# Turning the first q and k on the matrix engine and loading three batches ahead: sliding-window attention and a feed-forward layer

## The chip, the cores and the metric

The kernel runs on one core of a Trainium2 chip. The metric is the device time of one execution in microseconds (us). A core has five engines that work side by side, each in the order of its own instructions: PE (matrix multiply; its weight loads are shown apart as PEld), DVE (vector), ACT (scalar functions), POOL (general) and SP, which only issues transfers here. An engine starts an instruction when those that it needs on other engines have signalled, and everything behind it on the same engine waits with it. Transfers run on 16 DMA engines.

## The reference, cut to what matters

```python
# q, k, v: (8, 8, 576, 64) float32; w_in (512, 2048), w_out (2048, 512)
window, dilation = 32, 4
scores = 1/sqrt(64) * q @ k^T                       # per batch and head
rel = pos[:, None] - pos[None, :]
plain = (rel >= 0) & (rel < 32)                      # heads 0 to 3
dil   = (rel >= 0) & (rel < 128) & (rel % 4 == 0)    # heads 4 to 7
attn = softmax(where(mask, scores, -1e9)) @ v
x = attn.transpose(0, 2, 1, 3).reshape(4608, 512)
h = x @ w_in
out = maximum(0.01 * h, h) @ w_out                   # (4608, 512) float32
```

## The kernel before

**Attention.** The work is cut into 16 half-batches, called batches from here on and counted by `n`: four heads of one of the 8 batch entries, plain windows for even `n`, dilated ones for odd `n`. A batch has four units `u` (two pairs of heads, two halves of 288 tokens). `scores(u)` multiplies k by q on PE for both heads (six or eight small matmuls), takes the exponential on ACT (`er`) and the mask on DVE (`em`). `values(u)` multiplies by v (`o`) and by ones (`den`), takes the reciprocal (for units 0 to 7 as exp(-ln) on ACT, later on DVE) and writes `xT`, the attention output with the model dimension on the partitions, in float16. The tiles `sps`, `o` and `den` have one buffer each.

**Where q and k come from.** The scores need q and k with the head dimension on the partitions. `load(n)` brings q, k and v in float32, q and k in runs of one 64-element row (256 bytes); `cast(n)` turns them into float16 on POOL (two instructions each for q and k, one for v); `transpose(n)` has two DMA transposes write `qT` and `kT`, of which there are two sets, one for even and one for odd `n`.

**Feed-forward.** The 4608 tokens form nine chunks `c` of 512. A chunk has 32 pieces: 16 `ff_in` (four matmuls into `hp`, then a leaky relu on ACT into `gt`) and 16 `ff_out` (four matmuls each into `op`; after every fourth, ACT copies the result to `ob` and SP stores it). From chunk 0 on, a unit is woven into every four pieces: with piece `i` of chunk `c`, at `i % 4 == 0` come the scores of the next unit and, by the unit's place in its batch, the cast of the next batch, the load of the batch after it or the transpose of the next; at `i % 4 == 2` come the values. So chunks 0 to 6 hold eight units each (8 to 63), and units 0 to 7 run ahead of the feed-forward. A chunk needs the `xT` of its own 512 tokens. The eight weight blocks (1 MB each) are loaded into a staging tile with two buffers and cast on DVE.

**What sets the order.** The order is written out by hand: each engine takes its instructions in the order in which the program names them. SP issues everything from one queue: loads, transposes and output stores.

Of the kernel before, what the change touches and what calls it, by code (L numbers as in the profile page):

```python
# [14 lines left out]
WIN = 32  # L15
# [9 lines left out]
def _masks_np():  # L25
    krel = np.arange(128)[:, None]
    c = np.arange(S)[None, :]
    key = 96 * (c // 96) - 32 + krel
    rel = c - key
    plain = (key >= 0) & (rel >= 0) & (rel < WIN)  # L30
    tau, ql = c // HALF, c % 72
    uq = 72 * tau + ql
    uk = 72 * tau - 32 + krel
    dil = (uk >= 0) & (uq - uk >= 0) & (uq - uk < WIN)
    return np.concatenate([plain, dil], axis=1).astype(np.float16)


@with_exitstack
def kernel(ctx: ExitStack, tc: tile.TileContext, q, k, v, w_in, w_out, out):
# [12 lines left out]
    mask_d = nc.inline_tensor(_masks_np(), name="masks").ap()  # L52

# [3 lines left out]
    mask = cst.tile([128, 2, 2, HALF], FP16, name="mask")  # L57
    xT = cst.tile([128, 4, NTOK], FP16, name="xT")

    NQK = 3  # L60
    qT = [cst.tile([128, PAD + 2 * S + PAD], FP16, name=f"qT{i}") for i in range(2)]
    kT = [cst.tile([128, PAD + 2 * S + PAD], FP16, name=f"kT{i}") for i in range(2)]
# [10 lines left out]
    def load(n):  # L73
        b, kind = divmod(n, 2)
        base = (b * H + 4 * kind) * S * D
        for nm, x in (("q", q), ("k", k)):
            t = stg.tile([96, 24, D], FP32, tag=nm + "f")
            nc.sync.dma_start(t, rows_ap(x, base, [[D, 96], [96 * D, 24], [1, D]]))  # L78
            qkf[n, nm] = t
# [24 lines left out]
    def cast(n, eng):  # L104
        kind = n % 2
        for nm in ("q", "k"):
            t = att.tile([96, 2, 6, 2, D], FP16, tag=nm + "h")
# [6 lines left out]
        t = att.tile([128, 32, D], FP16, tag="vh")  # L114
        m = 32 if kind else 24
# [3 lines left out]
    def transpose(n):  # L119
        for nm, dst in (("q", qT), ("k", kT)):  # L120
            o = dst[n % 2][:, PAD:PAD + 2 * S].rearrange("p (c r) -> p c r", r=96)
            nc.sync.dma_start_transpose(  # L122
                o, qkh.pop((n, nm)).rearrange("p a t h d -> p (a t h d)"))

# [3 lines left out]
    def scores(u):  # L128
# [4 lines left out]
        for j in range(4 if kind else 3):  # L133
            w = 72 if kind else 96
            for hh in range(2):
                r = slice(64 * hh, 64 * hh + 64)
                if kind:
                    ka = kT[n % 2][r, tok - 128 + j: tok - 128 + j + 512: 4]
                    qa = qT[n % 2][r, tok + j: tok + j + 288: 4]
                else:  # L140
                    ka = kT[n % 2][r, tok + 96 * j - 32: tok + 96 * j + 96]
                    qa = qT[n % 2][r, tok + 96 * j: tok + 96 * j + 96]
# [4 lines left out]
        m = mask[:, kind, half, :]  # L147
        mb = bass.AP(tensor=m.tensor, offset=m.offset, ap=[m.ap[0], [0, 2], m.ap[1]])
        nc.vector.tensor_tensor(out=em, in0=er, in1=mb, op=ALU.mult)  # L149
# [53 lines left out]
    def ff_in(c, j):  # L203
        if j == 0:
            gts[c] = moe.tile([128, 16, CH], FP16, tag="gt", name="gt")
# [52 lines left out]
    cast(2, P)  # L258
    transpose(2)
    cast_w(0, 2, V)  # L260
    load_w(1, 0)
    cast_w(0, 3, V)
    load_w(1, 1)
    load(3)
    cast_w(1, 0, V)
    load_w(1, 2)
    cast_w(1, 1, V)
    load_w(1, 3)
    scores(8)
    NU = 8 * B  # L270
    u = 8
    for c in range(9):
        pieces = list(ff_pieces(c))
        for i, f in enumerate(pieces):
            if u < NU:
                if i % 4 == 0:
                    if u + 1 < NU:
                        scores(u + 1)
                    n = u // 4
                    if u % 4 == 0 and n + 1 < 2 * B:  # L280
                        cast(n + 1, P)
# [42 lines left out]
```

## Time and profile before

| | us |
|---|---|
| median of three timed runs | 433.36 (431.92 to 435.08) |
| the profiled execution | 427.88 |
| its span, first to last instruction | 426.1 |
| PE busy in the span | 326.3 (77%) |
| DVE busy | 190.8 (45%) |
| ACT busy | 152.0 (36%) |
| POOL busy | 80.9 (19%) |

The span is what the profile divides; 1.8 us of the profiled execution lie around it. A matmul is pipelined, so that busy time of PE is not all work. The granted clock is the share of PE's full clock that was given. In a group of instructions the columns are busy time and mean nanoseconds of one, then the idle time of the engine just before them and what ended it. In a chain and a timeline they are start, duration and what it was; a bracket gives the idle time before and its releaser. "L219" is line 219 of the kernel, and PE's names are those of the tiles.

### The profile page before, as it was taken

To read this page: it belongs to the slowest core of one execution; us is meant where nothing else is said; L and a number is where in the kernel's file an instruction comes from. 1 tells how busy PE (TensorE), PEld (TensorE's weight loads), DVE (VectorE), ACT (ScalarE), POOL (GpSimd) and SP (SyncE) were. 2 spreads that over 40 slices of the span, in tenths; PEclk is the share of its full clock that TensorE was granted. 3 is DMA by queue.
4 is the path that set the end of the run, shared out by engine and by line. 5 is a ranking of instruction groups with operands and counts; after the bars stand their busy time and mean duration, and the time that the engine had idled before them with its cause. 6 is when DMAs were issued, how large, how long until landed. Compare 5 with 4: busy or idle time off the path is not lost.

```text
span 426.1 us, 5328 instructions
## 1 busy us (share of the span) xinstructions
PE 326.3 (77%) x2176; PEld 138.0 (32%) x2176; DVE 190.8 (45%) x192; ACT 152.0 (36%) x261; POOL 80.9 (19%) x91
## 2 busy tenths in 40 slices
PE   0033455892999499958996799859894999999996
PEld 0022122340334134423342243314341444444442
DVE  0027355462567346653765366717571666400000
ACT  1044323420362136312641164206521562451631
POOL 4605033202131313131313131213111100000000
PEclk9999998898899879997999699969997999999999
DMA  9999999559482929192909291758366301101001
GB/s 215 268 281 282 231 305 330 101 132 209 94 172 67 272 63 205 37 263 67 240 12 259 69 234 33 183 157 201 65 142 196 82 0 51 50 2 74 25 26 74
DMA packets 154702, 61.43 MB, mean 144 GB/s; under 512 B 137677, under 2 KB 145845, under 8 KB 154677
## 3 DMA queue, kind: packets, MB, share of 16 engines
q1 hardware_dynamic: 154677, 61.09, 58.1%
q8 instruction: 17, 0.28, 0.3%
q14 instruction: 8, 0.07, 0.1%
HBM read 42.21 MB, written 9.44 MB: 121 GB/s over the span
## 4 chain that ended last, share of the span: by engine, by line
PE 45%; DMA 33%; SPq 9%; POOL 4%; ACT 3%; DVE 2%; issue 2%; POOLq 0%; ACTq 0%
PE op L219 24%; DMA t<-in_k_dram 19%; PE hp L208 15%; DMA kT<-t 13%; SPq L78 4%; POOL t L112 4%; PE sps L143 3%; PE o L163 2%; DMA t<-in_v_dram 2%; SPq L122 2%; ACT ob L223 2%; PE den L166 1%; SPq L224 1%; DVE w L198 1%; DVE xT L178 1%
## 5 line engine op out<-in xcount | busy, mean ns | idle before, releaser
L219 PE MATMUL op<-w,gt 128*128 128x512 f16 x576 | 144.8, 402 | 0.0
L208 PE MATMUL hp<-xT,w 128*128 128x512 f16 x576 | 139.1, 389 | 0.1
L174 DVE RECIPROCAL rec<-den 128x288 f32<-128x288 f32 x56 | 109.6, 1958 | 60.8 <-PE den L166 60.7
L210 ACT ACTIVATE gt<-hp 128x512 f16<-128x512 f32 x144 | 86.0, 597 | 63.1 <-PE hp L208 62.1
L143 PE MATMUL sps<-qT,kT 64*128 64x72 f16 (+1 forms) x448 | 25.3, 237 | 77.0 <-DMA kT<-t 74.5
L112 POOL CAST t<-t 96x768 f16<-96x768 f32 x64 | 52.7, 850 | 151.6 <-DMA t<-in_q_dram 137.6
L219 PEld LDWEIGHTS <-gt 128*128 128x128 f16 x576 | 54.0, 102 | 69.1 <-issue 12.2
L149 DVE TENSOR_TENSOR em<-er,mask 128x576 f16<-128x576 f16 x64 | 32.3, 506 | 95.1 <-ACT er L145 94.9
L208 PEld LDWEIGHTS <-w 128*128 128x128 f16 x576 | 52.7, 99 | 64.8 <-issue 5.9
L145 ACT ACTIVATE er<-sps 128x576 f16<-128x576 f32 x64 | 41.5, 649 | 71.7 <-PE sps L143 71.7
L223 ACT COPY ob<-op 128x512 f32<-128x512 f32 x36 | 21.1, 586 | 127.7 <-PE op L219 127.7
L143 PEld LDWEIGHTS <-kT 64*128 64x128 f16 x448 | 14.1, 111 | 103.2 <-DMA kT<-t 60.1
L116 POOL CAST t<-t 128x1536 f16<-128x1536 f32 (+1 forms) x16 | 26.9, 1682 | 99.6 <-PE o L163 48.6
L163 PE MATMUL o<-em,t 128*64 128x72 f16 (+1 forms) x448 | 22.4, 222 | 19.2 <-DVE xT L181 7.9
L163 PEld LDWEIGHTS <-t 128*64 128x64 f16 x448 | 14.6, 119 | 46.8 <-issue 29.1
L178 DVE TENSOR_TENSOR xT<-o,rec 128x288 f16<-128x288 f32 x32 | 25.6, 800 | 4.4 <-ACT rec L172 3.4
L166 PE MATMUL den<-em,ones 128*64 128x288 f16 x128 | 21.2, 322 | 0.0
L181 DVE TENSOR_TENSOR xT<-o,rec 128x288 f16<-128x288 f32 x32 | 14.6, 457 | 4.1 <-ACT rec L172 3.1
L198 DVE CAST w<-t 128x2048 f16<-128x2048 f32 x8 | 9.8, 1231 | 13.2 <-DMA t<-in_moe_w_out_dram 13.2
L166 PEld LDWEIGHTS <-ones 128*64 128x64 f16 x128 | 8.5, 124 | 0.0
L171 ACT ACTIVATE ln<-den 128x288 f32<-128x288 f32 x8 | 3.3, 411 | 7.7 <-PE den L166 7.7
L172 ACT ACTIVATE rec<-ln 128x288 f32<-128x288 f32 x8 | 3.5, 442 | 0.3
(10 smaller groups left out, 3.1 us busy)
## 6 DMA issues: line engine op xcount, KB each, us to landing
t<-in_q_dram SPq DMA_DIRECT2D x16, 576.0 KB, 4.9
t<-in_k_dram SPq DMA_DIRECT2D x16, 576.0 KB, 6.8
out_dram<-ob SPq DMA_DIRECT2D x36, 256.0 KB, 2.4
t<-in_v_dram SPq DMA_DIRECT2D x7, 1024.0 KB, 8.5
t<-in_v_dram SPq DMA_DIRECT2D x7, 768.0 KB, 7.4
t<-in_moe_w_in_dram SPq DMA_DIRECT2D x4, 1024.0 KB, 6.0
t<-in_moe_w_out_dram SPq DMA_DIRECT2D x4, 1024.0 KB, 7.7
t<-in_v_dram SPq DMA_DIRECT2D x1, 896.0 KB, 8.3
```

Source lines behind the costliest of these rows:

```text
L112: eng(out=dst, in_=src)
L143: nc.tensor.matmul(sps[:, hh, w * j:w * j + w], ka, qa, start=True, stop=True)
L145: nc.scalar.activation(out=er, in_=sps[:, :, 0:HALF], func=AF.Exp, scale=SCALE)
L149: nc.vector.tensor_tensor(out=em, in0=er, in1=mb, op=ALU.mult)
L163: nc.tensor.matmul(o[64 * hh:64 * hh + 64, w * j:w * j + w], vt[:, sl, :], em[:, hh, w * j:w * j + w], start=True, stop=True)
L166: nc.tensor.matmul(den[64 * hh:64 * hh + 64, 0:HALF], ones, em[:, hh, :], start=True, stop=True)
L174: nc.vector.reciprocal(out=rec, in_=den[:, 0:HALF])
L178: nc.vector.tensor_tensor(out=x, in0=o[:, 0:HALF].rearrange("p (r u) -> p r u", r=4), in1=rec.rearrange("p (r u) -> p r u", r=4), op=ALU.mult)
L208: nc.tensor.matmul(hp, w1[j // 4][:, i, 128 * (j % 4):128 * (j % 4) + 128], xT[:, i, CH * c:CH * c + CH], start=(i == 0), stop=(i == 3))
L210: nc.scalar.activation(out=gts[c][:, j, :], in_=hp, func=AF.Prelu, alpha=0.01)
L219: nc.tensor.matmul(op, gts[c][:, j, 128 * t:128 * t + 128], w2[j // 4][:, j % 4, :], start=(j == 0), stop=(j == 15))
L223: nc.scalar.copy(out=ob, in_=op)
```

## The change

Batches 0 to 3 (the first two batch entries) no longer go through the DMA transposes: their q and k are loaded so that a partition holds six neighbouring tokens of a head (runs of 1.5 KB), and `pe_transpose` turns each pair of heads by six PE transposes against an identity into a PSUM tile `tp`, from which DVE or ACT copies to `qT` or `kT`, putting the tokens back in order. There are three sets of `qT` and `kT` instead of two, three buffers for the cast v instead of two, and one instead of two for the cast q and k and for `gt`. From batch 4 on, `prefetch` names the load three batches ahead, the cast two ahead and the DMA transpose two ahead (before: two, one and one). The masks are built on POOL instead of loaded, in a smaller tile that is read with a stride of zero. Four of the eight weight casts move from DVE to POOL. In chunk 0 no unit is woven into the first 16 pieces; units 8 to 15 come with the last 16, one for every two pieces.

```diff
-    mask_d = nc.inline_tensor(_masks_np(), name="masks").ap()
-    mask = cst.tile([128, 2, 2, HALF], FP16, name="mask")
+    mask = cst.tile([128, 3, 96], FP16, name="mask")
+    nc.gpsimd.memset(mask, 1.0)
+    nc.gpsimd.affine_select(out=mask, in_=mask, pattern=[[0, 3], [1, 96]], base=32,
+                            channel_multiplier=-1, compare_op=ALU.is_ge, fill=0.0)
+    nc.gpsimd.affine_select(out=mask, in_=mask, pattern=[[0, 3], [-1, 96]], base=-1,
+                            channel_multiplier=1, compare_op=ALU.is_ge, fill=0.0)
+    nc.gpsimd.memset(mask[0:32, 0, :], 0.0)
+    ident = cst.tile([96, 96], FP16, name="ident")
+    nc.gpsimd.memset(ident, 0.0)
+    nc.gpsimd.affine_select(out=ident, in_=ident, pattern=[[-1, 96]], base=0,
+                            channel_multiplier=1, compare_op=ALU.not_equal, fill=1.0)
...
-            nc.sync.dma_start(t, rows_ap(x, base, [[D, 96], [96 * D, 24], [1, D]]))
+            if n < NPE:
+                nc.sync.dma_start(t.rearrange("p (h t) d -> p h (t d)", h=4),
+                                  rows_ap(x, base, [[6 * D, 96], [S * D, 4], [1, 6 * D]]))
+            else:
+                nc.sync.dma_start(t, rows_ap(x, base, [[D, 96], [96 * D, 24], [1, D]]))
...
+    def pe_transpose(n, p, nm, eng):
+        h = qkh[n, nm]
+        o = (qT if nm == "q" else kT)[n % NB][:, PAD + S * p:PAD + S * p + S]
+        tp = psm.tile([128, 1024], FP16, tag="pm", name="tp")
+        for t in range(6):
+            nc.tensor.transpose(tp[:, 96 * t:96 * t + 96],
+                                h[:, p, t].rearrange("p h d -> p (h d)"), ident)
+        eng(out=o.rearrange("p (r t) -> p t r", t=6),
+            in_=tp[:, 0:S].rearrange("p (t r) -> p t r", t=6))
...
     load(0)
-    nc.sync.dma_start(mask, mask_d.rearrange("p (a b c) -> p a b c", a=2, b=2))
     load(1)
-    cast(0, P)
-    transpose(0)
-    load_w(0, 0)
-    load_w(0, 1)
-    cast(1, P)
-    transpose(1)
-    load(2)
+    for g in range(4):
+        load_w(0, g)
+    cast_qk(0, V, A)
+    cast_v(0, P)
+    for p in range(2):
+        pe_transpose(0, p, "q", V)
+        pe_transpose(0, p, "k", A)
+    cast_qk(1, P, P)
+    cast_v(1, P)
     scores(0)
     scores(1)
     for u in range(8):
+        if u == 2:
+            for p in range(2):
+                pe_transpose(1, p, "k", A)
+                pe_transpose(1, p, "q", V)
         if u + 2 < 8:
             scores(u + 2)
         values(u, True)
         if u == 3:
-            cast_w(0, 0, V)
-            load_w(0, 2)
+            cast_w(0, 0, P)
         if u == 4:
             cast_w(0, 1, V)
-            load_w(0, 3)
+            load_w(1, 0)
+            load_w(1, 1)
+        if u == 5:
+            cast_w(0, 2, P)
...
+    load_w(1, 2)
     cast_w(0, 3, V)
+    load_w(1, 3)
+    load(2)
     load(3)
...
+    def prefetch(n, slot):
+        if slot == 0 and n + 3 < 2 * B:
+            load(n + 3)
+        if slot == 1 and NPE <= n + 2 < 2 * B:
+            cast_qk(n + 2, P, P)
+            cast_v(n + 2, P)
+        if slot == 3 and NPE <= n + 2 < 2 * B:
+            transpose(n + 2)
...
+            if c == 0:
+                if i in (2, 4, 6, 8):
+                    g = (i - 2) // 2
+                    cast_w(1, g, V if g % 2 else P)
+                if i == 10:
+                    cast_qk(2, V, P)
+                    cast_v(2, P)
+                if i == 12:
+                    load(4)
+                    pe_transpose(2, 0, "q", V)
...
+                if i == 15:
+                    pe_transpose(2, 1, "k", V)
+                    scores(8)
+                    cast_qk(3, P, P)
+                    cast_v(3, P)
+                if 17 <= i <= 20:
+                    pe_transpose(3, (i - 17) // 2, "kq"[(i - 17) % 2], V)
+                per = 2
+                go = i >= 16
+            else:
+                per = 4
+                go = True
+            if go and u < NU:
+                if i % per == 0:
+                    if u + 1 < NU:
+                        scores(u + 1)
+                    prefetch(u // 4, u % 4)
+                if i % per == per // 2:
+                    values(u, False)
+                    u += 1
             f()
```

**SP's queue in the chunks.** One chunk's worth of SP's rows in the kernel before, around chunk 2; the numbers tell the tiles apart, and the kind of v load (L85 even, L95 odd) tells the batch.

```order
L78 DMA t_897<-in_q_dram 96x24x64
L78 DMA t_899<-in_k_dram 96x24x64
L85 DMA t_901<-in_v_dram 128x24x64
L122 DMA_TRANSPOSE qT1_81<-t_840 128x12x96
L122 DMA_TRANSPOSE kT1_83<-t_843 128x12x96
L224 DMA out_0_dram<-ob_1093 128x512
L78 DMA t_1109<-in_q_dram 96x24x64
L78 DMA t_1111<-in_k_dram 96x24x64
L95 DMA t_1113<-in_v_dram 128x8x256
L224 DMA out_0_dram<-ob_1147 128x512
L122 DMA_TRANSPOSE qT0_80<-t_1053 128x12x96
L122 DMA_TRANSPOSE kT0_82<-t_1056 128x12x96
```

The same stretch of SP's queue in the changed kernel, from the load at a chunk's start on:

```order
L79 DMA t_1405<-in_q_dram 96x24x64
L79 DMA t_1407<-in_k_dram 96x24x64
L96 DMA t_1409<-in_v_dram 128x8x256
L124 DMA_TRANSPOSE qT2_91<-t_1460 128x12x96
L124 DMA_TRANSPOSE kT2_94<-t_1463 128x12x96
L79 DMA t_1618<-in_q_dram 96x24x64
L79 DMA t_1620<-in_k_dram 96x24x64
L86 DMA t_1622<-in_v_dram 128x24x64
L245 DMA out_0_dram<-ob_1656 128x512
L245 DMA out_0_dram<-ob_1712 128x512
L245 DMA out_0_dram<-ob_1760 128x512
L124 DMA_TRANSPOSE qT0_89<-t_1672 128x12x96
```

The second load now stands right behind the first pair of transposes, ahead of the chunk's first store, and the second pair stands behind the third store; each pair is for the batch after next, where before it was for the next.

**DVE in chunk 0.** DVE's rows before, from the first units after unit 7 on (`w2` are weight casts, `rec` the reciprocals):

```order
L174 RECIPROCAL rec_452<-den_443 128x288
L181 TENSOR_TENSOR xT_79<-o_442,rec_452 128x288
L198 CAST w2_2_94<-t_394 128x2048
L149 TENSOR_TENSOR em_477<-er_475,mask_78 128x576
L198 CAST w2_3_95<-t_397 128x2048
L174 RECIPROCAL rec_508<-den_499 128x288
L181 TENSOR_TENSOR xT_79<-o_498,rec_508 128x288
```

DVE's rows in the changed kernel from piece 17 of chunk 0 on; `tp` are the turned q and k of batch 3:

```order
L135 COPY kT0_92<-tp_647 128x6x96
L195 RECIPROCAL rec_665<-den_656 128x288
L202 TENSOR_TENSOR xT_88<-o_655,rec_665 128x288
L135 COPY qT0_89<-tp_672 128x6x96
L170 TENSOR_TENSOR em_689<-er_687,mask_78 128x576
L135 COPY kT0_92<-tp_703 128x6x96
L195 RECIPROCAL rec_721<-den_712 128x288
L202 TENSOR_TENSOR xT_88<-o_711,rec_721 128x288
L135 COPY qT0_89<-tp_731 128x6x96
```

The weight casts are gone from between these units, four copies out of PSUM have come in, and the units that were spread over 32 pieces now come within 16.

**POOL at the start.** POOL's rows in the changed kernel behind the common opening:

```order
L41 MEMSET ones 128x64
L44 MEMSET mask 128x288
L45 ISA
L45 AFFINE_SELECT mask<-mask 128x288
L47 AFFINE_SELECT mask<-mask 128x288
L49 MEMSET mask 32x96
L51 MEMSET ident 96x96
L52 AFFINE_SELECT ident<-ident 96x96
```

Before, the memsets of `kT`'s edges followed at once on that of `ones`; now the masks and the identity, with one ISA row, stand ahead of them and of every cast on POOL.

More of the change, by code (lines that the diff above doesn't have):

```diff
@@ L22 @@
 CH = 512
[L25 to L35, printed above, removed]
 @with_exitstack
@@ L277 @@
                     if u + 1 < NU:
                         scores(u + 1)
-                    n = u // 4
-                    if u % 4 == 0 and n + 1 < 2 * B:
-                        cast(n + 1, P)
-                    if u % 4 == 1 and n + 2 < 2 * B:
-                        load(n + 2)
-                    if u % 4 == 2 and n + 1 < 2 * B:
-                        transpose(n + 1)
-                if i % 4 == 2:
+                    prefetch(u // 4, u % 4)
+                if i % per == per // 2:
@@ L289 @@
             f()
-            if c == 0 and i == 3:
-                cast_w(1, 2, V)
-            if c == 0 and i == 5:
-                cast_w(1, 3, V)
 _INS = ['q', 'k', 'v', 'moe_w_in', 'moe_w_out']
```

64 lines of the change are left out of this document (32 added, 32 removed).

## The prediction

> **What bounds the kernel now.** I read the busy time by stages first. The cuts are the first score matmul (21.4), the first feed-forward matmul (50.2), the start of chunk 1 (112.4), of chunk 6 (333.1) and of chunk 7 (367.3).
>
> ```profile
> core 0: us, PE busy (x) PEld busy (x) DVE busy (x) ACT busy (x) POOL busy (x), PEclk, DMA share, GB/s
> 0.00:21.40 21.40, 0.00 (x0) 0.00 (x0) 0.00 (x0) 1.28 (x1) 10.76 (x20) 1.00 1.03 241
> 21.40:50.20 28.80, 9.50 (x141) 6.03 (x141) 14.61 (x20) 12.19 (x25) 5.43 (x5) 1.00 1.03 260
> 50.20:112.40 62.20, 42.03 (x260) 16.59 (x259) 29.20 (x29) 16.51 (x29) 14.86 (x15) 0.89 0.77 200
> 112.40:333.10 220.70, 185.29 (x1280) 75.97 (x1279) 122.42 (x121) 82.03 (x141) 49.90 (x51) 0.92 0.62 146
> 333.10:367.30 34.20, 34.20 (x247) 14.60 (x246) 23.59 (x23) 15.58 (x27) 0.00 (x0) 1.00 0.16 49
> 367.30:422.60 55.30, 55.24 (x256) 24.85 (x254) 0.95 (x2) 23.79 (x40) 0.00 (x0) 1.00 0.10 39
> ```
>
> From 333.1 on PE is busy all the time at full clock. Chunk 6 has eight units of attention in it like chunks 1 to 5 and takes 34.20 us, while those five take 220.70 / 5 = 44.14 us each, at a granted clock of 0.92. So no engine's work sets chunks 1 to 5; a wait does. The waits of PE between 112.4 and 333 have a single row:
>
> ```profile
> PE sps L143 <- DMA kT<-t: 35.3, 10, 6.9
> ```
>
> Ten waits, two a chunk, 7.1 us a chunk; the other 2.5 us or so are the slow matmuls after each long one (0.92). The chain of waits leads from there to POOL's cast of k and a load. SP's own rows tell it otherwise:
>
> ```profile
> 252.67 1.60 POOL L112 CAST t<-t 96x768 f16<-96x768 f32 x2 [0.34 <-DMA t<-in_k_dram]
> 267.39 0.37 SPq L224 DMA_DIRECT2D out_dram<-ob  x1
> 267.81 0.43 SPq L78 DMA_DIRECT2D t<-in_q_dram  x1
> 270.56 2.89 SPq L95 DMA_DIRECT2D t<-in_v_dram  x1
> 274.50 2.72 SPq L122 DMA_TRANSPOSE qT<-t  x1
> 277.31 2.55 SPq L122 DMA_TRANSPOSE kT<-t  x1
> 282.00 0.42 PE L143 MATMUL sps<-qT,kT 64*128 64x96 f16 x6 [6.43 <-DMA kT<-t]
> ```
>
> The k that PE waits for at 282.0 was cast by 254.3. Its transpose is issued only at 277.3, because SP works in order and stands first at an output store that PE must earn (267.4), then spends 5.7 us on the next load. The wait is made by the queue, not by bandwidth: the DMA share is 0.62.
>
> **The change, part by part.** *Chunks 1 to 5.* In the new order of SP each pair of transposes belongs to the batch after next. With T the start of a chunk: SP issues the load by T+5.7, and the pair behind it (274.50 to 282.0: 7.5 us from issue to use) is usable at T+13.2; its scores come at piece 28 of 32, T+30.3. The second pair stands behind three stores, the third ready at about T+30.9, so usable at T+38.4; its scores come at piece 12 of the next chunk, T+47.6. Margins of 17 and 9 us, where today there are none. What is late next: q and k now have one cast buffer, so a cast waits for the transposes of the batch before, and the loop of cast and transposes is 4 x 0.85 + 7.5 = 10.9 us against 17.3 us per batch. DVE has slack, as a steady unit shows:
>
> ```profile
> 162.25 0.29 PE L166 MATMUL den<-em,ones 128*64 128x288 f16 x2
> 162.58 1.96 DVE L174 RECIPROCAL rec<-den 128x288 f32<-128x288 f32 x1 [0.81 <-PE den L166]
> 164.57 0.46 DVE L181 TENSOR_TENSOR xT<-o,rec 128x288 f16<-128x288 f32 x1
> 166.36 0.32 PE L163 MATMUL o<-em,t 128*64 128x96 f16 x6
> ```
>
> xT ends at 165.03 and the next values start at 166.36: 1.3 us in hand. So I take these chunks to PE's floor: 34.20 and one score more (chunk 6 has seven; 0.42) is 34.6 us, a gain of 5 x (44.14 - 34.6) = 47.7 us. It cannot be more; it is nothing if the wait stays.
>
> *The head.* It ends with these rows:
>
> ```profile
> 4.93 1.59 POOL L112 CAST t<-t 96x768 f16<-96x768 f32 x2 [3.40 <-DMA t<-in_q_dram]
> 13.54 3.05 SPq L122 DMA_TRANSPOSE qT<-t  x1
> 21.44 0.42 PE L143 MATMUL sps<-qT,kT 64*128 64x96 f16 x6 [21.44 <-DMA kT<-t]
> 26.47 0.49 PE L166 MATMUL den<-em,ones 128*64 128x288 f16 x2
> 31.06 0.44 PE L143 MATMUL sps<-qT,kT 64*128 64x72 f16 x8 [4.09 <-DMA kT<-t]
> 46.14 0.80 DVE L178 TENSOR_TENSOR xT<-o,rec 128x288 f16<-128x288 f32 x1 [1.70 <-ACT rec L172]
> 50.20 3.60 PE L208 MATMUL hp<-xT,w 128*128 128x512 f16 x8
> 367.29 13.81 PE hp L208 x64
> DMA packets 3322, 0.85 MB, mean 282 GB/s; under 512 B 3322, under 2 KB 3322, under 8 KB 3322
> DMA packets 836, 1.68 MB, mean 336 GB/s; under 512 B 16, under 2 KB 16, under 8 KB 836
> L198 DVE CAST w<-t 128x2048 f16<-128x2048 f32 x8 | 9.8, 1231 | 13.2 <-DMA t<-in_moe_w_out_dram 13.2
> L112 POOL CAST t<-t 96x768 f16<-96x768 f32 x64 | 52.7, 850 | 151.6 <-DMA t<-in_q_dram 137.6
> L116 POOL CAST t<-t 128x2048 f16<-128x2048 f32 x8 | 15.2, 1895 | 61.0 <-PE o L163 48.6 <-PE den L166 10.9 <-DMA t<-in_v_dram 1.5
> L64 POOL MEMSET kT<- 128x128 f16 x2 | 0.4, 205 | 0.0
> L145 ACT ACTIVATE er<-sps 128x576 f16<-128x576 f32 x64 | 41.5, 649 | 71.7 <-PE sps L143 71.7
> t<-in_moe_w_in_dram SPq DMA_DIRECT2D x4, 1024.0 KB, 6.0
> ```
>
> The loads: 0.59 MB of q take 2.1 us at 282 GB/s (256-byte runs, 11 to 14 us) and 1.75 at 336 (2 KB runs, 50 to 55 us); 1.5 KB lies between, nearer the second. So q lands at 4.6 instead of 4.93, k at 6.4. ACT casts k in 2 x 0.87 (649 ns by 768/576), to 8.1. PE's transposes aren't in the trace. Their nearest rows are the scores: six with a weight load each take 0.42 us, so 24 take 1.7 if they pipeline and 24 x 0.24 = 5.7 if not; I take the first and 0.9 for the last copy, 2.6 us a batch. A copy of 128x576 out of PSUM lies between er's 0.65 and that by the ratio of the two xT (0.80 scattered against 0.46), 1.14; I take 0.9. The first scores then start at about 10.0 (8.8 to 12) instead of 21.44. On POOL the masks are three selects, each between a memset's 0.2 us and a cast's 0.85; done by 4 us, they lie beside the load. The mask's own load, 0.29 MB, goes.
>
> A rule speaks against it: the Trainium skill's "GPSIMD Engine Reference" (2.1, Instruction dispatch) gives about 6 us for the first call of a freshly loaded kernel, and POOL has a new ISA row ahead of its first select. By that estimate the identity would come near 10 us and the scores 2.5 us later, 362 in all; no run here shows it. The Trainium skill's "TensorE: Matmul & The Clock Gate" (Part 4: PE-mode transpose) gives about 275 ns for one PE transpose inside a kernel; worked out from it as an estimate, 24 take 6.6 us, which would add some 12 us over batches 0 to 2 and end at 372. Here too no run shows one yet.
>
> *Units 0 to 7.* Unit 1's den ends 5.5 us after the first score (26.96 against 21.44); the transposes of batch 1 follow, 2.6, where today PE sits 4.09 for kT. Scores(4) start 8.1 us after the first, today 9.6. From there to the last xT it is 15.9 us (31.06 to 46.94), less one weight cast that leaves DVE (1.23): 10.0 + 8.1 + 14.7 = 32.8. Scores(8) no longer stand ahead, so the feed-forward starts near 33 instead of 50.2.
>
> *Chunk 0.* Its 64 first matmuls take 13.8 us, and 1.9 more for the cold start (3.60 for eight against 1.73). Piece 12 would come at 45.3 but waits for batch 2: load(2) now stands behind eight weight loads in two buffers, so from the third on each waits for a cast: 6.0 us to land and 1.2 (DVE) or 1.9 (POOL) to cast. w_in's third is issued near 21, its fourth after unit 4 near 27, w_out's first near 28, its second after unit 7 near 34, its fourth near 41 to 42; q of batch 2 lands near 48.5 and is cast by 49.5. Cost 4 us, plus 1.5 for k, cast by POOL behind it, and 2.6 of transposes: piece 16 at 57. Then eight units go at twice the pace, and PE (two pieces of 0.86 and (34.6 - 55.3/2) / 8 = 0.87 for the unit, 2.6 us) no longer sets it. The buffer of o is single, so the chain den, reciprocal, xT, next o does: 1.96 + 0.46 to 0.80 + 0.45 + 0.15 of gaps, 3.0 to 3.4 us a unit. With 2.4 to the first den, 7 x 3.2, 2.8 behind the last and 4 copies of batch 3 at 0.9, chunk 1 starts at about 89 (80 to 97) instead of 112.4: gain 23.4.
>
> **Sum**, against the profiled execution's 427.88: 427.9 - 47.7 - 23.4 = 356.8. Chunks 6 to 8 and the end stay. The timed median, 433.36, is 1.3% above that execution; by the same ratio 361, so I say 360.
>
> **The rivals.** *The wait stays.* If the transposes, queued behind a 2 MB load, land after their scores as before, only the head's gain is left: 427.9 - 23.4 = 404.5, by the same ratio 410; half of the wait gives 384. For it: SP stays one queue. Against: margins of 9 and 17 us.
>
> *POOL and DVE get in each other's way.* One row speaks for it, an em of 1.73 us beside POOL's cast, where the mean is 0.51:
>
> ```profile
> 39.47 1.47 POOL L116 CAST t<-t 128x1536 f16<-128x1536 f32 x1 [0.96 <-DMA t<-in_v_dram]
> 39.51 1.73 DVE L149 TENSOR_TENSOR em<-er,mask 128x576 f16<-128x576 f16 x1
> L149 DVE TENSOR_TENSOR em<-er,mask 128x576 f16<-128x576 f16 x64 | 32.3, 506 | 95.1 <-ACT er L145 94.9
> ```
>
> In steady chunks the 1.3 us in hand swallow the 1.2. In chunk 0's second half nothing does, and POOL casts three batches there: 4 to 8 units at 1.2 are 5 to 10 us, 365 to 370. PE transposes that don't pipeline (5.7 a batch instead of 2.6) would add 9.3 us for batches 0 to 2, and with both it is 380.
>
> *Slower than before.* The loop over the single cast buffer: cast(n+2) waits until transposes(n+1) have landed, and they wait for cast(n+1) behind SP's loads. It decides from 17.3 us a batch. To end at 437 or more the ten batches of chunks 1 to 5 must lose 7.7 us each, a loop of 25.0 us, a transpose pair of 21.6 instead of 7.5. No row is near it.
>
> *The change doesn't do what it says.* Should 1.5 KB runs move no faster, each q or k lands 0.35 us later, 1 us in the head: inside the range.
>
> **How the numbers follow.** Forecast, 346 to 368: 0.68. Contention or slow transposes, 368 to 382: 0.15. Half or more of the wait left, 382 to 409: 0.07. Below 346, chunk 0's chain shorter than I make it: 0.06. Within 1% (what a measurement of this kernel can tell from no change): 0.02. Slower by more: 0.02. The range 346 to 382 holds 0.83; its lower end is chunk 1 at 80 (348) less a little, its upper end the loss of half the steady gain. Faster by over 1%: 0.96.
>
> **What the new profile would show.** Right: no row kT in PE's waits between chunks 1 and 5, chunks of about 34.6 us at a clock near 1.00, first score near 10, first feed-forward matmul near 33, chunk 1 near 89 with DVE nearly full before it. Wrong: chunks still near 44 with sps waiting for kT; an idle PE before piece 12 much longer than 5 us; the first select ending near 8 us; em rows over 1 us throughout.

## The result, and the profile after

The changed kernel takes 369.52 us (median of four runs, 367.16 to 369.74) beside 432.64 for the kernel before: a ratio of 0.851 (95% interval 0.846 to 0.857). The forecast was 360 with a range of 346 to 382. The profiled execution took 367.16 us with a span of 365.5, beside 427.88 and 426.1 before.

The busy time by stages of the changed kernel is cut at these events: first score 12.7, first feed-forward matmul 36.3, piece 16 of chunk 0 62.7, the end of PE's wait at the start of chunk 1 98.5, chunk 6 272.0, chunk 7 306.2. (In the kernel before, the cut for chunk 1, 112.4, lies 0.4 us behind its first feed-forward matmul; here 98.5 lies 1.8 us behind it.) The columns are those of the first table of the prediction.

```profile
12.70:36.30 23.60, 10.66 (x152) 7.53 (x152) 14.38 (x19) 15.99 (x25) 9.33 (x8) 1.00 0.74 247
36.30:62.70 26.40, 18.85 (x103) 8.32 (x102) 11.60 (x10) 10.52 (x19) 7.65 (x7) 0.87 0.93 276
62.70:98.50 35.80, 26.31 (x222) 10.99 (x221) 34.36 (x31) 8.14 (x14) 15.53 (x16) 0.90 1.15 263
98.50:272.00 173.50, 173.36 (x1278) 73.12 (x1278) 123.66 (x120) 80.34 (x139) 49.14 (x51) 1.00 0.75 173
272.00:306.20 34.20, 34.20 (x247) 14.60 (x246) 23.75 (x23) 15.59 (x27) 0.00 (x0) 1.00 0.10 35
```

Chunks 1 to 5 take 173.50 us, 34.70 each, with PE busy all the time at full clock; before they took 220.70. That is 47.2 us of the 60.6 us by which the span shrank. The start of chunk 1 at 98.5 instead of 112.4 gives 13.9 more (15.3 by its first feed-forward matmul, 96.7 instead of 112.0), and what follows chunk 5 is 0.5 us longer than before. Ahead of chunk 1 the table shows two new limits: in 62.7 to 98.5 DVE is busy 34.36 of 35.80 us, and in the stretch before it PE is idle for 7.6 of 26.4 us.

PE's waits between 98.5 and 272 (total, times, longest) are a single row, and kT isn't in it:

```profile
PE hp L229 <- DVE xT L199: 0.9, 1, 0.9
```

SP's rows in one chunk show why. The timeline's columns are start, duration and what it was:

```profile
168.03 0.34 SPq L245 DMA_DIRECT2D out_dram<-ob  x1
168.42 0.42 SPq L79 DMA_DIRECT2D t<-in_q_dram  x1
170.97 2.14 SPq L96 DMA_DIRECT2D t<-in_v_dram  x1
173.21 2.98 SPq L124 DMA_TRANSPOSE qT<-t  x1
176.29 2.76 SPq L124 DMA_TRANSPOSE kT<-t  x1
179.10 0.57 SPq L79 DMA_DIRECT2D t<-in_q_dram  x1
```

The pair of transposes still stands behind 4.8 us of load issue, as before. But its batch is used half a chunk later, so nobody waits.

### The profile page after: what moved, and what is told of

Same layout as the page of the kernel before. It is cut to its first block, busy times and chain, and to the rows that moved or that the text cites. A ratio compares the mean times of both kernels' runs of the same rounds, so it can differ in the third digit from the quotient of the medians.

```text
span 365.5 us, 5534 instructions
## 1 busy us (share of the span) xinstructions
PE 320.9 (88%) x2272; PEld 141.3 (39%) x2272; DVE 213.5 (58%) x204; ACT 160.0 (44%) x267; POOL 86.1 (24%) x97
## 4 chain that ended last, share of the span: by engine, by line
PE 72%; DVE 11%; DMA 5%; ACT 5%; SPq 3%; issue 2%; POOL 0%; POOLq 0%; ACTq 0%
PE hp L229 31%; PE op L240 31%; DVE rec L195 5%; PE o L184 4%; PE sps L156 4%; DMA t<-in_k_dram 4%; SPq L76 3%; DVE xT L199 2%; PE den L187 2%; ACT kT L135 2%; DMA t<-in_moe_w_out_dram 1%; DVE qT L135 1%; ACT rec L193 1%; ACT ln L192 1%; DVE xT L202 1%
## 5 line engine op out<-in xcount | busy, mean ns | idle before, releaser
L229 PE MATMUL hp<-xT,w 128*128 128x512 f16 x576 | 137.0, 385 | 1.5 <-DVE xT L199 1.3
L240 PE MATMUL op<-w,gt 128*128 128x512 f16 x576 | 137.9, 385 | 0.0
L112 POOL CAST t<-t 96x768 f16<-96x768 f32 x58 | 48.8, 876 | 137.8 <-DMA qT<-t 122.7
L240 PEld LDWEIGHTS <-gt 128*128 128x128 f16 x576 | 51.6, 98 | 62.2 <-issue 2.3
L165 DVE TENSOR_TENSOR em<-er,mask 128x576 f16<-128x576 f16 x48 | 27.1, 564 | 13.7 <-ACT er L158 13.3
L156 PE MATMUL sps<-qT,kT 64*128 64x72 f16 (+1 forms) x448 | 24.4, 231 | 6.3 <-ACT er L158 3.4
L184 PEld LDWEIGHTS <-t 128*64 128x64 f16 x448 | 13.9, 115 | 39.3 <-issue 13.3
L133 PE MATMUL tp<-ident,t 96*128 96x96 f16 x96 | 8.5, 256 | 18.1 <-DVE t L112 14.2
L135 DVE COPY qT<-tp 128x576 f16<-128x576 f16 x8 | 16.6, 2116 | 1.8 <-PE tp L133 1.8
L133 PEld LDWEIGHTS <-t 96*128 96x128 f16 x96 | 7.0, 126 | 22.0 <-DVE t L112 14.6
L219 POOL CAST w<-t 128x2048 f16<-128x2048 f32 x4 | 7.6, 1893 | 21.7 <-DMA t<-in_moe_w_out_dram 15.9
```

The lines of the kernel that those rows point to most:

```text
L112: eng(out=dst, in_=src)
L135: eng(out=o.rearrange("p (r t) -> p t r", t=6), in_=tp[:, 0:S].rearrange("p (t r) -> p t r", t=6))
L156: nc.tensor.matmul(sps[:, hh, w * j:w * j + w], ka, qa, start=True, stop=True)
L165: nc.vector.tensor_tensor(out=em.rearrange("p h (t c) -> p (h t) c", c=w), in0=er.rearrange("p h (t c) -> p (h t) c", c=w), in1=mb, op=ALU ...
L184: nc.tensor.matmul(o[64 * hh:64 * hh + 64, w * j:w * j + w], vt[:, sl, :], em[:, hh, w * j:w * j + w], start=True, stop=True)
L229: nc.tensor.matmul(hp, w1[j // 4][:, i, 128 * (j % 4):128 * (j % 4) + 128], xT[:, i, CH * c:CH * c + CH], start=(i == 0), stop=(i == 3))
```

## The experiments

The first table has the times of all kernels that ran, with their ratio to the kernel before in the same series. The last three columns are from the profiled execution: the start of chunk 1's first feed-forward matmul, that of chunk 7's, and a sixth of what lies between. (In the changed kernel that first matmul comes 1.8 us ahead of the cut at 98.5: after three matmuls PE waits for the last `xT`.)

| kernel | median us | ratio (95%) | chunk 1 | chunk 7 | one chunk |
|---|---|---|---|---|---|
| before | 432.64 | 1 | 112.0 | 367.1 | 42.5 |
| the change | 369.52 | 0.851 (0.846 to 0.857) | 96.7 | 306.0 | 34.9 |
| e3: the change with the old lead | 423.59 | 0.981 (0.975 to 0.987) | 102.7 | 362.2 | 43.3 |
| e4: before, two lines exchanged | 371.56 | 0.860 (0.855 to 0.866) | 102.1 | 310.6 | 34.7 |
| e12: before, transposes a unit earlier | 431.11 | 0.987 (0.980 to 0.994) | 114.6 | 372.0 | 42.9 |
| e13: before, load a unit later | 381.42 | 0.874 (0.867 to 0.881) | 101.7 | 319.7 | 36.3 |
| e1: copy not scattered | 356.93 | 0.827 (0.823 to 0.832) | 85.6 | 295.6 | 35.0 |
| e9: scattered on the read side | 358.88 | 0.824 (0.817 to 0.831) | 85.8 | 295.1 | 34.9 |
| e2: 256-byte rows, copy not scattered | 359.78 | 0.834 (0.829 to 0.838) | 89.6 | 299.3 | 34.9 |
| e6: load(2) ahead of w_out | 372.50 | 0.861 (0.856 to 0.865) | 101.0 | 310.3 | 34.9 |
| e7: logarithm for units 8 to 15 | 361.65 | 0.836 (0.832 to 0.841) | 93.7 | 302.9 | 34.9 |
| e8: e2, e6 and e7 together | 357.54 | 0.825 (0.820 to 0.830) | 87.6 | 296.4 | 34.8 |
| e10: e2 and e7 together | 357.78 | 0.824 (0.816 to 0.831) | 86.4 | 294.6 | 34.7 |
| e11: e8, and batch 2 cast earlier | 356.26 | 0.819 (0.813 to 0.824) | 87.0 | 295.2 | 34.7 |

### Is it the order of SP? The old lead in the new kernel (e3)

```diff
-        if slot == 0 and n + 3 < 2 * B:
-            load(n + 3)
-        if slot == 1 and NPE <= n + 2 < 2 * B:
-            cast_qk(n + 2, P, P)
-            cast_v(n + 2, P)
-        if slot == 3 and NPE <= n + 2 < 2 * B:
-            transpose(n + 2)
+        if slot == 0 and NPE <= n + 1 < 2 * B:
+            cast_qk(n + 1, P, P)
+            cast_v(n + 1, P)
+        if slot == 1 and NPE < n + 2 < 2 * B:
+            load(n + 2)
+        if slot == 2 and NPE <= n + 1 < 2 * B:
+            transpose(n + 1)
```

> The changed kernel with the old lead from batch 4 on: cast of the next batch, load of the one after next, DMA transpose of the next, at the old places; everything else as changed. Theory: the lead alone took the wait for kT away. Then the wait comes back, some 7 us a chunk, chunks 1 to 5 take 43 to 45 us instead of 34.7, and the time is 408 to 418. Rival: the lighter queue of the changed kernel (three buffers, fewer transposes) is enough: chunks below 38, time below 385.

Measured: 423.59 us. All else of the change in place, the chunks are back at 43.3 us, and PE's waits have their row again, eight times from chunk 1 to chunk 6:

```profile
PE sps L156 <- DMA kT<-t: 39.2, 8, 8.0
```

So what chunks 1 to 5 gained goes when the old places and the old lead of loads, casts and transposes come back; the other parts of the change don't bring it without them. I had expected a few us less, since I kept the gain of the head whole; chunk 1 itself comes 6 us later with the old lead.

### The order alone, without the lead (e4, e12, e13)

Three kernels exchange or move statements of the kernel before. e4 names the transposes of the next batch in the slot of the load, and the load in theirs:

```diff
-                    if u % 4 == 1 and n + 2 < 2 * B:
-                        load(n + 2)
-                    if u % 4 == 2 and n + 1 < 2 * B:
-                        transpose(n + 1)
+                    if u % 4 == 1 and n + 1 < 2 * B:
+                        transpose(n + 1)
+                    if u % 4 == 2 and n + 2 < 2 * B:
+                        load(n + 2)
```

> The kernel before with one exchange: within a batch the DMA transposes of the next batch are named ahead of the load of the batch after it (places 1 and 2 exchanged). No tile, buffer or lead changes otherwise. Theory: the wait was made by SP's queue, transposes standing behind an output store and 5.7 us of load issue. Then most of the wait goes: 0 to 2 us a chunk instead of 7.1, chunks 1 to 5 at 34.7 to 37, time 383 to 396 against 427.9 to 433. Rival: the chain of waits is right and the wait comes from load and cast, one batch ahead being too little: chunks stay at 43 to 46, time 425 to 440.

Measured: 371.56 us, better than expected. From chunk 1 to chunk 6 no wait of PE is left. The stage table of e4 (cut at 102.1 and 310.5) has PE at full clock throughout:

```profile
102.10:310.50 208.40, 208.19 (x1528) 87.97 (x1525) 150.93 (x143) 96.99 (x167) 53.20 (x54) 1.00 0.72 168
```

An exchange of two statements does nearly what the whole change does (0.860 against 0.851; the intervals overlap). The expectation left chunk 0 out: there the kernel before has the same wait for kT, 8.1 us long and ended at 105.8, and chunk 1 of e4 starts at 102.1 instead of 112.0. SP's rows of e4 show one of the two pairs of a chunk right behind the store that PE earns, ahead of the next load:

```profile
194.39 0.36 SPq L224 DMA_DIRECT2D out_dram<-ob  x1
194.86 1.33 SPq L122 DMA_TRANSPOSE qT<-t  x1
196.29 1.27 SPq L122 DMA_TRANSPOSE kT<-t  x1
198.80 0.36 SPq L224 DMA_DIRECT2D out_dram<-ob  x1
199.21 1.01 SPq L78 DMA_DIRECT2D t<-in_q_dram  x1
```

The exchange does two things at once: the transposes are a unit earlier, and the load is out of their way. Two more kernels take them apart. e12 names the transposes a unit earlier but behind the load (`u % 4 == 1` for both):

> The kernel before, with the transposes named one unit earlier, right behind the load instead of a unit later. Theory (SP's order): the pair still stands behind a store of PE and 5.7 us of load issue; only the second store leaves its way. It is issued at 273.45 instead of 274.50 in the stretch shown, so the wait of 6.4 us a chunk becomes about 5.5: 422 to 428 profiled, chunks of about 43. Rival: that the exchange gained so much because the transposes were named a unit earlier; then this kernel takes 372 (368 to 376) as the exchange did, with no wait for kT in the chunks.

e13 leaves the transposes where they were and names the load behind them (`u % 4 == 3`):

> The kernel before, with the transposes named where they were and the load a unit later, so behind them. Theory (SP's order): the pair no longer stands behind the load but still behind the second store, which PE earns a unit after the first (4.3 us): issue at about 271.7 instead of 274.5, use at 279.2 instead of 282.0, so 3.6 us of the 6.4 stay in the second pair and nothing of the first: chunks of 38 to 39, 402 (392 to 412). Rival one: only the place in units counts; nothing changes, 428 to 436. Rival two: only the load's issue counts; no wait is left, 370 to 376.

Measured: e12 431.11 us, e13 381.42. PE's waits for kT from chunk 1 on, of e12 and then of e13:

```profile
PE sps L143 <- DMA kT<-t: 37.7, 10, 7.0
```

```profile
PE sps L143 <- DMA kT<-t: 7.6, 5, 2.2
```

A unit of lead with the load ahead takes nothing off the wait; the load out of the way takes most of it off. So it is the load ahead of the pair, as the prediction read it. Whether the pair waits for SP, which issues the load first, or for the DMA engines, which carry it first, these runs don't tell: in the kernel before, the engines have no work from 263.0 to 267.4 and are busy at a share of 0.59 to 1.24 from 267.4 to 282.0. The mean of 0.62, by which the prediction ruled bandwidth out, hides this. That the traffic as a whole isn't too much is shown: without the wait the share is 0.72 (e4) and 0.75 (the change). The size was wrong in e13, where I had expected 3.6 us a chunk and 1.3 to 2.2 were left. Its rows tell the rest:

```profile
235.44 4.76 SPq L224 DMA_DIRECT2D out_dram<-ob  x2
240.31 1.32 SPq L122 DMA_TRANSPOSE qT<-t  x1
241.73 1.31 SPq L122 DMA_TRANSPOSE kT<-t  x1
244.96 0.30 PE L143 MATMUL sps<-qT,kT 64*128 64x96 f16 x6 [1.34 <-DMA kT<-t]
```

With no load just ahead, the pair takes 4.65 us from its issue to its use (240.31 to 244.96), and SP 1.3 us for each of the two. Behind a load it took 7.5 us and 2.5 to 2.7. So the load costs the pair twice: its own issue, and 2.9 us in the pair itself.

### Where the missing 9.5 us are: the copies out of PSUM (e1, e9)

The groups of the changed kernel that have `tp` (busy, mean ns of one, then idle before):

```profile
L135 DVE COPY qT<-tp 128x576 f16<-128x576 f16 x8 | 16.6, 2116 | 1.8 <-PE tp L133 1.8
L135 DVE COPY kT<-tp 128x576 f16<-128x576 f16 x4 | 8.5, 2123 | 0.3 <-PE tp L133 0.2
L135 ACT COPY kT<-tp 128x576 f16<-128x576 f16 x4 | 8.0, 2189 | 0.0
L133 PE MATMUL tp<-ident,t 96*128 96x96 f16 x96 | 8.5, 256 | 18.1 <-DVE t L112 14.2 <-ACT t L112 2.2 <-POOL t L112 1.8
```

A copy takes 2.1 us; I had 0.9. e1 copies without putting the tokens back in order (the tokens of batches 0 to 3 come out in another order, and their scores with them):

```diff
-        eng(out=o.rearrange("p (r t) -> p t r", t=6),
-            in_=tp[:, 0:S].rearrange("p (t r) -> p t r", t=6))
+        eng(out=o, in_=tp[:, 0:S])
```

> The changed kernel, with the copies out of PSUM written in a row instead of scattered with a step of six tokens; tokens of batches 0 to 3 are then out of order, which this run leaves so. Theory: the copies are what the prediction sized wrong (2.1 us each in place of 0.9) and most of chunk 1's lateness (98.5 against 89) hangs on them. Then a flat copy takes 0.65 to 0.8 us, the first score comes at about 11.4 us instead of 12.8, and chunk 1 starts at 88 to 91: 357 to 360 us against 367.2. Rival: the copies lie beside other work, and the weight loads ahead of batch 2 set chunk 0: 364 to 367.

Measured: 356.93 us, with copies of 455 ns (DVE) and 638 (ACT). Chunk 1 starts 11.1 us earlier than with the change (10.4 by the end of PE's wait there, 88.1 against 98.5). e9 keeps the order of the tokens, but moves the stride from the output to the input of the copy:

```diff
-        eng(out=o.rearrange("p (r t) -> p t r", t=6),
-            in_=tp[:, 0:S].rearrange("p (t r) -> p t r", t=6))
+        eng(out=o.rearrange("p (r t) -> p r t", t=6),
+            in_=tp[:, 0:S].rearrange("p (t r) -> p r t", t=6))
```

> As the changed kernel with its 1.5 KB runs, but the copy out of PSUM writes qT and kT in order without gaps and takes its input with a stride instead (96 halfwords apart, six at a time). If the 2.1 us of a copy come from 2-byte writes that are scattered in the SBUF tile, this copy takes the 0.46 us (DVE) and 0.64 us (ACT) of the copy that is not scattered at all, and the kernel takes its time, 357 us (354 to 360). If the scattered access costs the same on either side, a copy stays at 2.1 us and the kernel at 369.5 (367 to 372). Half of it on the read side: a copy of 1.1 to 1.3 us, 361 to 364.

Measured: 358.88 us, the time of e1 within the intervals, with these groups:

```profile
L135 DVE COPY qT<-tp 128x576 f16<-128x576 f16 x8 | 6.0, 754 | 3.9 <-PE tp L133 3.9
L135 DVE COPY kT<-tp 128x576 f16<-128x576 f16 x4 | 3.0, 756 | 3.4 <-PE tp L133 3.4
L135 ACT COPY kT<-tp 128x576 f16<-128x576 f16 x4 | 2.5, 635 | 0.5 <-PE tp L133 0.3
```

The same reordering takes 2.1 us where the write is scattered, and 0.75 (DVE) or 0.64 (ACT) where the read is. On ACT the scattered read is as cheap as none at all. The side of the copy that has the stride is worth some 11 us, without any change of what is computed.

### Are 1.5 KB runs faster? (e2)

e2 has the copy of e1, and loads batches 0 to 3 in rows of 256 bytes as all others are; their tokens then come out in order.

> As the run with flat copies, but q and k of batches 0 to 3 loaded in 256-byte runs (one row a partition), by which the tokens are in order again with flat copies. Theory: the 1.5 KB runs bring nothing (by 8 us 1.46 MB had come in with them, 1.54 MB before), and by this run the first cast of q starts at 5 to 6 us instead of 6.4 and the time is that of the flat copies within 2 us. Rival: short runs cost bandwidth as the prediction had it, the eight loads each come 0.35 us later or more, and piece 12 of chunk 0 waits 2 to 4 us longer: 2 to 4 us above the run with flat copies.

Measured: 359.78 us. The first casts of q (DVE) and of k (ACT), which start when the loads have landed, first of the changed kernel, then of e2:

```profile
6.40 1.02 DVE L112 CAST t<-t 96x768 f16<-96x768 f32 x2 [6.40 <-DMA t<-in_q_dram]
8.96 1.56 ACT L112 CAST t<-t 96x768 f16<-96x768 f32 x2 [6.87 <-DMA t<-in_k_dram]
```

```profile
5.34 1.02 DVE L108 CAST t<-t 96x768 f16<-96x768 f32 x2 [5.34 <-DMA t<-in_q_dram]
7.56 1.56 ACT L108 CAST t<-t 96x768 f16<-96x768 f32 x2 [5.47 <-DMA t<-in_k_dram]
10.00 0.42 PE L151 MATMUL sps<-qT,kT 64*128 64x96 f16 x6 
```

At the start of the kernel q lands 1.1 us later with the longer runs and k 1.4, and e2 has its first score 2.8 us ahead of the changed kernel; 1.6 of these are the copy, since e1, with the longer runs and the copy of e2, has it at 11.19. The run length is not the only difference: with the longer runs SP has issued q, k and v by 2.7 us, with the short rows by 5.7, so q and k share the engines with v sooner. In the first 10 us 1.97 MB come in for e1 and 2.10 for e2. So the longer runs bring no gain here; why they land later stays open.

e2 doesn't keep its lead: its median is 2.9 us above e1's. PE waits for the kT of batch 4 ahead of chunk 1, a wait that e1 has with 1.0 us and e2 with 3.8. SP's rows of e2 show the old pattern once more, the pair behind a load:

```profile
67.72 2.52 SPq L75 DMA_DIRECT2D t<-in_q_dram  x1
72.35 1.91 SPq L92 DMA_DIRECT2D t<-in_v_dram  x1
75.50 5.12 SPq L120 DMA_TRANSPOSE qT<-t  x1
80.72 2.50 SPq L120 DMA_TRANSPOSE kT<-t  x1
85.28 0.40 PE L151 MATMUL sps<-qT,kT 64*128 64x96 f16 x6 [3.82 <-DMA kT<-t]
```

The intervals of the two ratios overlap (0.823 to 0.832 and 0.829 to 0.838), but the times in the same series don't (356.7 to 358.5 and 359.6 to 360.5). The rival's 2 to 4 us above e1 came, but not by its reason: the loads come earlier, and the wait is for kT of batch 4.

### The wait ahead of piece 12, and DVE's chain (e6, e7)

Two places of chunk 0 waited longer than the prediction had it. In the changed kernel PE waits 7.1 us for the q of batch 2, and the chain of `o` holds it behind:

```profile
52.69 1.23 DVE L219 CAST w<-t 128x2048 f16<-128x2048 f32 x1 [7.02 <-DMA t<-in_moe_w_out_dram]
55.00 1.02 DVE L112 CAST t<-t 96x768 f16<-96x768 f32 x2 [1.08 <-DMA t<-in_q_dram]
55.61 0.66 PE L133 MATMUL tp<-ident,t 96*128 96x96 f16 x6 [7.14 <-DVE t L112]
76.58 0.45 PE L184 MATMUL o<-em,t 128*64 128x96 f16 x6 [3.23 <-DVE xT L202]
```

e6 names `load(2)` ahead of the four loads of `w_out` instead of behind them.

> The changed kernel with the load of batch 2 named ahead of the four w_out loads instead of behind them. Theory: PE's 7.1 us before piece 12 of chunk 0 are the two-buffer chain of weight loads and casts that q of batch 2 stands behind. Then q of batch 2 is cast before PE comes to piece 12 at 48.5, that wait goes, and chunk 1 starts 5 to 8 us earlier (90 to 94): 359 to 363. Rival: the transfers are limited by bandwidth there (DMA share 0.93), and w_out comes as much later as q comes earlier: PE waits for w_out at pieces 16 to 19 instead, time 365 to 368.

Measured: 372.50 us, not faster. The theory fell, and the time lies above the rival's too: PE now waits 10.7 us there instead of 7.1. e6's rows on DVE:

```profile
57.20 1.49 DVE L219 CAST w<-t 128x2048 f16<-128x2048 f32 x1 [5.68 <-DMA t<-in_moe_w_out_dram]
58.62 2.27 DVE L112 CAST t<-t 96x768 f16<-96x768 f32 x2
60.48 0.66 PE L133 MATMUL tp<-ident,t 96*128 96x96 f16 x6 [10.68 <-DVE t L112]
```

The load came earlier, but its cast stands on DVE behind the fourth cast of `w_out`, and that block now lands later by the time of the load. So the wait goes by everything that DVE has to do ahead of that cast, not by the load of batch 2 alone.

e7 takes the reciprocals of units 8 to 15 on ACT, as units 0 to 7 have them.

```diff
-                    values(u, False)
+                    values(u, u < 16)
```

> The changed kernel with the reciprocals of units 8 to 15 taken as exp(-ln) on ACT, as for units 0 to 7, instead of on DVE. Theory: the second half of chunk 0 (35.8 us from piece 16 to chunk 1) goes by the chain den, reciprocal, xT, next o on DVE, 3.0 to 3.4 us a unit, with four copies on top. Then a unit costs PE's 2.6 us or little more and the half takes 26 to 30 us: time 360 to 362. Rival: the half is held by loads and casts of batches 3 to 5 (POOL busy 15.5 of 35.8): less than 2 us gained.

Measured: 361.65 us (0.836, 0.832 to 0.841), 8 us below the change. e7's rows at the wait ahead of piece 12, at piece 16 and at the start of chunk 1:

```profile
57.79 0.66 PE L133 MATMUL tp<-ident,t 96*128 96x96 f16 x6 [8.76 <-DVE t L112]
66.02 1.04 PE L240 MATMUL op<-w,gt 128*128 128x512 f16 x4
93.67 2.18 PE L229 MATMUL hp<-xT,w 128*128 128x512 f16 x8
```

From piece 16 to the first matmul of chunk 1 it is 27.7 us, within the 26 to 30 expected, where the change takes 34.0 (62.67 to 96.72). DVE is busy for 20.1 us of it instead of 32.6: its chain was the bound there. The profiled execution of e7, the slowest of its four (364.01 us), shows only 3.2 us of the gain, since in it the wait ahead of piece 12 is 8.8 us instead of 7.1 and piece 16 comes 3.3 us later.

### Together (e8, e10, e11)

e8 is e2, e6 and e7 in one.

> 256-byte runs with flat copies, the load of batch 2 ahead of w_out, and exp(-ln) for units 8 to 15, all in one; output in order. Theory: the three costs lie one behind the other (copies 8 us, the wait before piece 12 some 7, the chain 6 to 8), and most of them adds: chunk 1 at 75 to 82, time 343 to 351. Rival: one cover hides the others (what stays is the bandwidth of 25 MB in the first 75 us), and the time is that of the best of the three alone, 355 to 360.

e10 leaves e6 out again:

> 256-byte rows for batches 0 to 3 with copies out of PSUM that are not scattered, and the reciprocals of units 8 to 15 as exp(-ln) on ACT. Theory: the two gains lie in different places (copies ahead of the first scores and of piece 16; the chain of DVE in the second half of chunk 0, where reciprocals of 1.96 us stand), so that most of the 8 us of the second adds to the first's 359.8: 352 (349 to 356), chunk 1 at 82 to 85. Rival: the cast of k for batch 5, which waited until the transposes of batch 4 had landed and cost 3.8 us in the run without the logarithm, takes the place of DVE's chain: 356 to 360, with a wait of sps for kT of 6 us or more.

e11 is e8 with the casts of batch 2 named at piece 1 instead of 10, ahead of the casts of `w_out`, and two buffers for the cast q and k:

> As the kernel with 256-byte rows, copies not scattered and the logarithm for units 8 to 15, and besides: load(2) is named ahead of the loads of w_out, the casts of batch 2 ahead of the casts of w_out (piece 1 instead of 10), and the cast q and k have two buffers. Theory: an earlier load of batch 2 gained nothing before because its cast stood behind w_out's casts on DVE and POOL, which the load had made later; with the cast ahead of them no transpose of batch 2 waits over 1 us and chunk 1 starts near 80 (76 to 84): 348 (345 to 352). Rival: w_out, now 4.5 us later, is waited for by the first feed-forward outputs instead: piece 16 to 19 stand still for 4 to 8 us, 352 to 357.

Measured: 357.54, 357.78 and 356.26 us. All three theories fell, and the rivals had the sizes right. The gains don't add; with e1 and e9 there are five kernels within 3 us, and chunk 1 starts between 85.6 and 87.6 in all of them. In e8 PE waits 11.7 us ahead of piece 12; in e10 the wait for kT of batch 4 is 3.5 us, not the 6 that its rival named. e11 has the lowest median, but its interval overlaps those of e8, e9 and e10. What holds e11 are two waits of PE in chunk 0:

```profile
56.18 0.42 PE L151 MATMUL sps<-qT,kT 64*128 64x96 f16 x6 [6.43 <-DVE kT L131]
82.72 0.30 PE L151 MATMUL sps<-qT,kT 64*128 64x96 f16 x6 [4.30 <-DMA kT<-t]
```

At 56.2 the copies of batch 2 stand on DVE behind the fourth cast of `w_out` (54.16 to 55.39): the wait of e6 has moved from the cast to the copy. At 82.7 it is the pair of batch 4 again, issued from 74.8 on behind a load (65.8 to 73.6); a second cast buffer, which e11 has, doesn't take that wait away. So e11's rival was right in size (352 to 357), but not in place. The pair of batch 4 ahead of that load, and the copies of batch 2 ahead of that cast, were not tried. Nor was it shown how far the DMA engines themselves bound chunk 0; their share is 1.15 at 263 GB/s in its second half (62.7 to 98.5 of the changed kernel).

## Why the prediction was right, and where it was off

**Chunks 1 to 5: right in mechanism and size.** 34.6 us were forecast for each and 34.70 measured; the gain was 47.2 us, not 47.7. That the place of the transposes behind a load in SP's queue makes the wait was read from SP's rows, and e3, e4, e12 and e13 show it. "Not by bandwidth" was argued from a mean share and is shown only for the traffic as a whole (0.75 and no wait); while the pair waits, the DMA engines are busy at 0.59 to 1.24. What I didn't see is that the lead of a batch isn't needed: e4 has the old lead and no wait. And the transposes' price of 7.5 us, which I took as fixed, is 4.65 without a load ahead of it (e13).

**Chunk 1 at 89: off by 9.5 us** (98.5; 7.7 by its first matmul). The same steps in the forecast, in the changed kernel, and in e9, which differs from it by the copy alone:

| step, us | forecast | the change | e9 |
|---|---|---|---|
| first score | 10.0 | 12.8 | 11.1 |
| from there to scores(4) | 8.1 | 10.1 | 8.0 |
| first feed-forward matmul | 32.8 | 36.3 | 31.9 |
| PE's wait ahead of piece 12 | 4 | 7.1 | 4.7 |
| piece 16 | 57 | 62.7 | 57.4 |
| chunk 1 | 89 | 98.5 | 87.6 |

```profile
50.03 0.66 PE L133 MATMUL tp<-ident,t 96*128 96x96 f16 x6 [4.72 <-DVE t L112]
87.58 1.24 PE L229 MATMUL hp<-xT,w 128*128 128x512 f16 x5 [0.93 <-DVE xT L199]
```

With the cheap copy every step comes within 1.4 us of its forecast. One by one:

- *First score at 10.0; it came at 12.78.* q was to land at 4.6 and k at 6.4, as a gain of the longer runs; q's cast started at 6.40 and k's at 8.96. The step read a speed by run length off loads of other places in the program. e2, with the short rows and a cheap copy, lands earlier and has its first score at 10.00; e1, with the long runs and the same copy, at 11.19.
- *A copy of 0.9 us between bounds of 0.65 and 1.14; it took 2.1.* This is the term that failed. The upper bound carried the ratio of the two `xT` (0.80 against 0.46) over. But the scattered `xT` writes every fourth halfword and costs 0.34 us / 288 = 1.2 ns an element more than the plain one, while the copy writes every sixth and costs (2.12 - 0.455) / 576 = 2.9 ns an element more. A row with another stride was taken for a bound, and it is none. Why the price grows so was not measured, nor whether it is the write or the memory that sets it (e9 strides a read of PSUM, the change a write to SBUF). The two copies that follow one another on ACT (10.54 to 14.54) and two on DVE make the head 2 us longer ahead of scores(4), and the four of batch 3 fill DVE in the second half.
- *24 transposes in 2.6 us with their last copy: the PE part was nearly right.* The row of batch 1:

```profile
19.37 2.10 PE L133 MATMUL tp<-ident,t 96*128 96x96 f16 x24
```

  24 take 2.10 us, 0.09 each, where 1.7 was expected. The Trainium skill's "TensorE: Matmul & The Clock Gate" (Part 4: PE-mode transpose) has about 275 ns for one; the listed mean here is 256, but they overlap, so that the estimate of 6.6 us worked out from it did not come about.
- *Feed-forward at 32.8; it came at 36.3.* 2.8 us from the first score and 2.0 up to scores(4); from there to here it was 1.3 faster than forecast.
- *Piece 12 to wait 4 us; it waited 7.1.* The fourth block of `w_out` was to be issued near 41 to 42 and q of batch 2 cast by 49.5; it was cast from 55.00 on. In e9 it is cast from 49.41 on and the wait is 4.7, so most of the miss hangs on the copies, by which the head and the weight loads behind it come later.
- *The second half of chunk 0 in 32 us; it took 35.8.* The chain of `o` was named rightly (e7). The units without copies run at 3.1 to 4.2 us, near the 3.0 to 3.4 of the forecast, while the first ones share DVE with the four scattered copies; in e9 the half takes 30.2. The forecast's own terms, 2.4 + 22.4 + 2.8 + 3.6 = 31.2, lead from 57 to 88.2, not 89.

**Masks on POOL: right.** The selects take 0.44 us:

```profile
1.30 0.44 POOL L45 TENSOR_SCALAR_AFFINE_SELECT mask<-mask 128x288 f16<-128x288 f16 x1
2.66 0.26 POOL L52 TENSOR_SCALAR_AFFINE_SELECT ident<-ident 96x96 f16<-96x96 f16 x1
```

The identity is there at 2.9 us. Of the 6 us that the Trainium skill's "GPSIMD Engine Reference" (2.1, Instruction dispatch) has for the first call of a freshly loaded kernel, this execution shows nothing.

**The total** is 9.5 us above the forecast by the medians, and 10.4 by the profiled executions (367.16 against 356.8): 9.5 in front of chunk 1, 0.5 in chunks 1 to 5 and 0.5 behind them. With the copy near its forecast price (e9) the kernel takes 358.88 us against 360 forecast; that the late loads and the longer wait at piece 12 don't show there is luck, since the way from scores(4) to the feed-forward is 1.9 us shorter than forecast and the second half of chunk 0 1.8. Of the rivals, contention had the right figures (365 to 370) with the wrong reason: em rows over 1 us are there, but only two in that half (1.07 us at 64.67 and 1.70 at 87.36), and the copies and not POOL fill DVE, as e9 shows.

## What to carry to other kernels

Where one engine issues all transfers in order, look at what stands ahead of the late one in its queue before buying buffers or lead: exchanging two statements gave a ratio of 0.860 where the whole change gave 0.851. Let a copy that reorders 2-byte elements gather on its read side and write without gaps, and time it (0.75 us instead of 2.1 here). And an earlier load gains nothing while its cast, or the copy behind it, stands in order behind something late: e6 moved the load alone, e11 the load and the cast, and each time the wait went on to what came next.

## What the runs showed of the hardware

- A copy of 128x576 halfwords from PSUM takes 0.46 us (DVE) and 0.64 (ACT) plain, 0.75 and 0.64 with a strided read (96 halfwords apart, e9), and 2.1 and 2.2 with the same reordering as a strided write to SBUF (six halfwords apart).
- A DMA transpose takes SP 1.3 us to issue with no load just ahead of it (e4, e13) and mostly 2.3 to 5.2 right behind one (the kernel before, the change, e2, e12), and the pair's time from issue to use grows from 4.65 to 7.5 us.
- In the first 10 us of the kernel, q and k in runs of 1.5 KB landed 1.0 to 1.4 us later than in rows of 256 bytes, with v issued sooner behind them.
- 24 PE transposes of 96x128 take 2.10 us in a row, 0.09 each, though each is listed with 256 ns.
